# A fused attention and feed-forward kernel: two batches' state reads late, the second batch's first product kept on chip, the opening in another order

## The chip, the core and the metric

The kernel runs on one core of a Trainium2 chip. The metric is the device time of one execution in microseconds; a profiled execution also has a span, which is the time from its first to its last recorded instruction. The core has five engines, each with its own queue that runs in order: PE (matmul), DVE (VectorE), ACT (ScalarE), POOL (GpSimd) and SP, which here only issues DMA transfers.

## The reference

Both halves are in float32. For each of 8 batches and 8 heads, attention runs between 512 tokens `x` and 32 state rows, in both directions; the results, `xread` (512 rows) and `sread` (32 rows), are the input of a feed-forward layer of width 2048.

```python
scores = scale * np.matmul(x, state.transpose(0, 1, 3, 2))
scores = scores - scores.max(-1, keepdims=True)
a = np.exp(scores)
a /= a.sum(-1, keepdims=True) + 1e-09
xread = np.matmul(a, state)
scores2 = scale * np.matmul(state, x.transpose(0, 1, 3, 2))
# the same softmax over scores2 gives a2
sread = np.matmul(a2, x)
...
h = x @ w_in            # x: the (8 * 544) x 512 rows of both reads
g = h - np.tanh(h)
return g @ w_out
```

The weights arrive in float64, and the kernel takes their two 32-bit halves apart itself.

## The kernel before

**The main loop.** The rows are worked in nine chunks: chunk i below 8 is batch i's `xread`, chunk 8 is all `sread`. A chunk has 16 steps f, one for each block of 128 hidden columns: `hidden(f)` multiplies into a bank of PSUM, `finish` takes tanh on ACT and the difference on DVE and splits it into two parts `g` (the upper part by a copy on ACT, the rest by a subtraction on DVE, both in `split`, lines 90 and 91), and `output(f)` adds twelve matmuls of `g` with `wo`, the split block of `w_out` (lines 413, 414 and 415). `xread` is never formed: `m = state * w_in` is made for each batch, so that `hidden` is `a * m`.

**The products m.** For batches 0 and 1 they come from float32 matmuls with `w_in` blocks as they are converted (`m_first_two`, and letters m, k and R of the opening). The lower 64 partitions of the result are batch 0's and are copied into the SBUF tile `m_first`; the upper 64 are batch 1's and go through a tile `st` and a DMA into a DRAM tile `md`, from which `load_m` fetches them as `mr`. Batches 2 to 7 are made later, in `m_units`, and also pass through `md`.

**The weights.** Each of the 32 weight blocks (`w00d` to `w33d`, `wo0d` to `wo15d`, 512 KB each) is loaded into one of five raw tiles, converted by three DVE instructions (lines 120, 121, 124) and one on ACT (line 123), and then, for `w_out`, split (line 90 on ACT, 91 on DVE). `w_in` blocks are also written to DRAM as `wf` for later use. All loads are issued by SP, and a load waits until the conversion of an earlier block has freed its raw tile.

**The opening.** The string `SEQ` is an order written by hand. Its letters are one step each: S scores matmul, c copy of the scores to SBUF, T transpose, M maximum, B or q subtraction of the maximum (B on DVE, q on POOL), E exponential, Z, N and A normalization and transpose back, a, b, r and p the four conversion steps of a `w_in` block, m and k the product and its copy for batch 0, h and H the first hidden matmuls, X and G `finish`, D a matmul with zeros that writes nothing of use.

**State read.** `state_read(b)` computes batch b's `sread` from the copy `s` of its scores. For each half it has, on DVE, a maximum (line 306), small instructions on single columns (308, 312, 313) and four scalings (335); on ACT an exponential (310) and a copy (321); on PE four transposes (319) and its matmuls (329); on SP the load of `xn` (316).

**What sets the order elsewhere.** `SCH` is a table of step numbers st = 16 i + f: "conv", "pair" and "wo" for the weights, "a0" for batch 0's state read, "att0" and so on for the attention of later batches, "m0" and "m1" for the units of m. A planner then places instructions within an engine; `issue_after` keeps a piece from being placed ahead of another one.

Of the kernel before, what the change touches and what calls it, by code (L numbers as in the profile page):

```python
# [19 lines left out]
P = 128  # L20
# [5 lines left out]
SCALE = 1.0 / D**0.5  # L26
EPS = 1e-9
LAG = 2
LONE = 2


@with_exitstack
def attention_ffn(ctx: ExitStack, tc: tile.TileContext, xT, xn, bd, bh, sp, sm, sl, win, wout, xout, sout):
# [105 lines left out]
    WSUB = nc.gpsimd if None else None  # L139
    XSUB = nc.gpsimd if '1' else None  # L140

    def m_first_two(q, p):

        k, c = p // 2, p % 2
        if p == 0:

            m_first[q] = pool.tile([P, 2, 512], F32, tag="mr", name=f"mr0{q}", bufs=RRB)
        ps = bank(ps_a, f"mps0{q}{p}")
        nc.tensor.matmul(ps, sps[:, p], wfs[q, k][:, c], start=True, stop=True)
        nc.scalar.copy(m_first[q][64 * c : 64 * c + 64, k], ps[0:64])  # L150
        stage = pool.tile([P, 2, 512], F32, tag="stage", name=f"st0{q}{p}", bufs=SB)
        nc.scalar.copy(stage[64:128, 0], ps[64:128])
        nc.sync.dma_start(
            mdram[1][q][0][k, 2 * c : 2 * c + 2].rearrange("h n f -> (h n) f"), stage[64:128, 0]
        )

    def m_units(g):

# [33 lines left out]
                    yield  # L192

    def load_m(b, q):
        if b == 0:
            r = m_first[q]
        else:
            r = pool.tile([P, 2, 512], F32, tag="mr", name=f"mr{b}{q}", bufs=RRB)
            addends = mdram[b][q]
            nc.sync.dma_start(r, addends[0].rearrange("g h n f -> (h n) g f"))  # L200
            if len(addends) > 1:
                r2 = pool.tile([P, 2, 512], F32, tag="stage", name=f"ml{b}{q}", bufs=SB)
                nc.sync.dma_start(r2, addends[1].rearrange("g h n f -> (h n) g f"))
# [29 lines left out]
    def attention(b, aT):  # L233


        if b < LONE:
            bdr = pool.tile([P, 4, 64], F32, tag="bdr", name=f"bdr{b}", bufs=1)
        else:
            bdr = pool.tile([P, 4, NS], F32, tag="bdr", name=f"bdr{b}", bufs=1)
        with tc.issue_after(loadlog[min(len(loadlog) - 1, XH1)]):  # L240
            nc.sync.dma_start(bdr, bd[b] if b < LONE else bh[b - LONE])
        xrs, ss, es = [], [], []
        for hf in range(2):
            xr = pool.tile([P, 2, 512], F32, tag="x", name=f"xT{b}{hf}", bufs=XB)
            with tc.issue_after(loadlog[min(len(loadlog) - 1, XH1)]):
                nc.sync.dma_start(xr, xT[b, hf])
            xrs.append(xr)
        yield
        pss = {}

        def scores(hf):
            pss[hf] = bank(ps_a, f"sps{b}{hf}")
            for c in range(2):
                nc.tensor.matmul(pss[hf][64 * c : 64 * c + 64], bdr[:, 2 * hf + c], xrs[hf][:, c], start=True, stop=True)

        def all_scores():

            pss.update({hf: bank(ps_a, f"sps{b}{hf}") for hf in range(2)})
            for j in range(4):
                for hf in range(2):  # L260
                    rs = slice(64 * hf, 64 * hf + 64)
                    nc.tensor.matmul(  # L262
                        pss[hf][32 * j : 32 * j + 32], bdr[rs, j], xrs[j // 2][rs, j % 2], start=True, stop=True
                    )

        if b >= LONE:
            all_scores()
        for hf in range(2):
# [218 lines left out]
    EARLY = int('0')  # L487
# [22 lines left out]
    def step(op):  # L510
# [5 lines left out]
            for c in range(2):  # L516
                o(nc.tensor.matmul(sps_ps[j][64 * c : 64 * c + 64], bdr[:, 2 * j + c], xrs[j][:, c], start=True, stop=True))
        elif k == "c":
            ss[j] = pool.tile([P, 512], F32, tag="s", name=f"s0{j}")
            o(nc.scalar.copy(ss[j], sps_ps[j]))  # L520
        elif k == "T":
            es[j] = pool.tile([P, 512], F32, tag="e", name=f"e0{j}")
# [57 lines left out]
            chunks[0].g[j] = g  # L580
        elif k == "R":

            if j % 2 == 0:
                stages[j // 2] = pool.tile([P, 4, 256], F32, tag="stage", name=f"st00{j}", bufs=SB)
            st = stages[j // 2]
            with tc.issue_after(tanhs[RE[j]][0]):
                nc.scalar.copy(st[64:128, :, P * (j % 2) : P * (j % 2) + P], mps[j][64:128])
            if j % 2:
                for k in range(2):
                    nc.sync.dma_start(  # L590
                        mdram[1][0][0][k, :, :, P * (j - 1) : P * (j + 1)].rearrange("(c h) n f -> (h n) c f", c=2),
                        st[64:128, 2 * k : 2 * k + 2],
                    )
# [51 lines left out]
    for i in range(B + 1):  # L645
        for f in range(NFF):
# [19 lines left out]
                chunks[i + 1].hidden(nf - NFF)  # L666
            for _ in range(D0["pair"].count(st)):
                m_first_two(*next(pairs))
            with tc.issue_after(first):
                advance(a0, D0["a0"].count(st))  # L670
            for b in range(1, B):
                n = D0["att"][str(b)].count(st)
                if n:
                    if b not in atts:
                        atts[b] = new_attention(b)
                    advance(atts[b], n)
            for g in range(2):
                advance(m1[g], D0[f"m{g}"].count(st))
# [50 lines left out]
```

## Time and profile before

| what | value |
|---|---|
| device time, 3 runs | 687.70, 688.42, 689.92 us; median 688.42 |
| the profiled execution | 688.88 us, span 687.1 us, mean granted PE clock 0.988 |
| busy in the span | PE 96%, DVE 67%, ACT 55%, POOL 1% |
| DMA over the span | 99.30 MB |
| first matmul of chunk 0's output | at 32.9 us |
| last matmuls' copy out | from 683.4 us |

Matmul records overlap, so "96%" is not a rate: in the middle of the program a matmul of 512 columns starts every 0.23 us, though each record lasts 0.39. The first 140 us differ from the rest, and the views below are of that part.

### The profile page before, as it was taken

To read this page: it belongs to the slowest core of one execution; us is meant where nothing else is said; L and a number is where in the kernel's file an instruction comes from. 1 tells how busy PE (TensorE), PEld (TensorE's weight loads), DVE (VectorE), ACT (ScalarE), POOL (GpSimd) and SP (SyncE) were. 2 spreads that over 40 slices of the span, in tenths; PEclk is the share of its full clock that TensorE was granted. 3 is DMA by queue.
4 is the path that set the end of the run, shared out by engine and by line. 5 is a ranking of instruction groups with operands and counts; after the bars stand their busy time and mean duration, and the time that the engine had idled before them with its cause. 6 is when DMAs were issued, how large, how long until landed. Compare 5 with 4: busy or idle time off the path is not lost.

```text
span 687.1 us, 9286 instructions
## 1 busy us (share of the span) xinstructions
PE 660.5 (96%) x3386; PEld 521.7 (76%) x3386; DVE 458.2 (67%) x803; ACT 377.9 (55%) x663; POOL 6.6 (1%) x11
## 2 busy tenths in 40 slices
PE   4788988999999999999999999999999999999997
PEld 2446666888788887888788878887878788888896
DVE  5897999965695559556876568546853587434442
ACT  3768876766675655457656555634433354333342
POOL 2100000000000000000000000000000000000000
PEclk9899998999999999999999999999999999999999
DMA  8888972555545552345536432643241312001310
GB/s 292 252 300 257 340 275 93 183 185 144 169 122 188 150 168 97 124 126 162 175 124 203 133 106 86 220 145 127 89 157 44 124 48 95 28 14 41 131 32 31
DMA packets 46317, 99.30 MB, mean 145 GB/s; under 512 B 6208, under 2 KB 12096, under 8 KB 46272
## 3 DMA queue, kind: packets, MB, share of 16 engines
q1 hardware_dynamic: 46272, 98.72, 44.4%
q8 instruction: 26, 0.43, 0.3%
q14 instruction: 19, 0.16, 0.1%
HBM read 66.72 MB, written 31.98 MB: 144 GB/s over the span
## 4 chain that ended last, share of the span: by engine, by line
PE 85%; DMA 6%; DVE 4%; ACT 3%; issue 1%; SPq 0%; ACTq 0%; DVEq 0%
PE ops L413 17%; PE ops L414 17%; PE ops L415 17%; PE hps L376 9%; PE hps L377 9%; PE hps L375 9%; PE mps L187 2%; PE sps L262 1%; PE rps L329 1%; DMA mr<-md 1%; PE mps L186 1%; DMA w01d<-in_win 1%; DMA wf<-w 1%; PE pps L319 1%; DMA w31d<-in_win 1%; DMA wo1d<-in_wout 1%
## 5 line engine op out<-in xcount | busy, mean ns | idle before, releaser
L414 PE MATMUL ops<-wo,g 128*128 128x512 f32 x544 | 215.5, 396 | 2.1 <-DVE wo L91 2.1
L413 PE MATMUL ops<-wo,g 128*128 128x512 f32 x544 | 208.1, 397 | 3.1 <-ACT wo L90 3.1
L415 PE MATMUL ops<-wo,g 128*128 128x512 f32 x544 | 208.4, 394 | 0.0
L383 DVE TENSOR_TENSOR t<-hps,t 128x512 f32<-128x512 f32 (+1 forms) x142 | 93.3, 658 | 98.4 <-ACT t L383 97.5
L383 ACT ACTIVATE t<-hps 128x512 f32<-128x512 f32 (+1 forms) x142 | 81.1, 573 | 133.7 <-PE hps L377 131.4
L413 PEld LDWEIGHTS ops<-wo,g 128*128 128x128 f32 x544 | 102.4, 189 | 32.1 <-ACT wo L90 5.8
L90 ACT CAST g<-t 128x512 fp32r<-128x512 f32 (+1 forms) x142 | 84.6, 596 | 72.9 <-DVE t L383 56.6
L414 PEld LDWEIGHTS ops<-wo,g 128*128 128x128 f32 x544 | 103.2, 190 | 26.5 <-DVE wo L91 3.3
L91 DVE TENSOR_TENSOR g<-t,g 128x512 fp32r<-128x512 f32 (+1 forms) x142 | 93.3, 657 | 42.4 <-ACT g L90 41.1
L415 PEld LDWEIGHTS ops<-wo,g 128*128 128x128 f32 x544 | 102.8, 189 | 24.5 <-issue 2.4
L375 PE MATMUL hps<-aT,m 128*128 128x512 f32 x248 | 98.3, 397 | 0.0
L377 PE MATMUL hps<-aT,m 128*128 128x512 f32 x248 | 97.1, 393 | 0.6 <-DVE m L91 0.6
L376 PE MATMUL hps<-aT,m 128*128 128x512 f32 x248 | 97.0, 391 | 0.0
L377 PEld LDWEIGHTS hps<-aT,m 128*128 128x128 f32 x248 | 46.7, 188 | 11.0 <-DVE m L91 1.0
L91 DVE TENSOR_TENSOR wst<-w,wst 64x512 fp32r<-64x512 f32 x64 | 43.9, 686 | 16.4 <-ACT wst L90 15.0
L375 PEld LDWEIGHTS hps<-aT,m 128*128 128x128 f32 x248 | 46.6, 188 | 10.5 <-issue 0.7
L376 PEld LDWEIGHTS hps<-aT,m 128*128 128x128 f32 x248 | 46.7, 188 | 10.0 <-issue 0.5
L91 DVE TENSOR_TENSOR m<-mr,m 128x1024 fp32r<-128x1024 f32 x31 | 37.8, 1220 | 9.3 <-ACT m L90 8.6
L188 ACT COPY st<-mps 128x512 f32<-128x512 f32 x64 | 36.7, 587 | 12.3 <-PE mps L187 12.0
L90 ACT CAST wst<-w 64x512 fp32r<-64x512 f32 x64 | 39.6, 619 | 1.8 <-ACT wo13r L123 1.0
L90 ACT CAST m<-mr 128x1024 fp32r<-128x1024 f32 x31 | 32.3, 1043 | 7.3 <-DMA mr<-md 7.2
L187 PE MATMUL mps<-wst,sms 128*128 128x512 f32 x64 | 24.7, 394 | 0.0
(218 smaller groups left out, 587.6 us busy)
## 6 DMA issues: line engine op xcount, KB each, us to landing
md<-st SPq DMA_DIRECT2D x144, 128.0 KB, 2.2
mr<-md SPq DMA_DIRECT2D x28, 512.0 KB, 4.0
xT<-in_xT SPq DMA_DIRECT2D x16, 512.0 KB, 4.6
xn<-in_xn SPq DMA_DIRECT2D x16, 512.0 KB, 4.2
w<-wf SPq DMA_DIRECT2D x16, 512.0 KB, 4.6
out_x<-ob SPq DMA_DIRECT2D x32, 256.0 KB, 2.1
wn<-wf SPq DMA_DIRECT2D x8, 512.0 KB, 3.8
ml<-md SPq DMA_DIRECT2D x8, 512.0 KB, 3.6
```

The costliest lines, as they stand in the source:

```text
L90: nc.scalar.copy(hi, src)
L91: return (sub or nc.vector).tensor_sub(lo, src, hi)
L186: nc.tensor.matmul(ps, s[:, 1, h], t[:, e], start=True, stop=False)
L187: nc.tensor.matmul(ps, s[:, 0, h], t[:, e], start=(g == 1), stop=True)
L188: nc.scalar.copy(stage[:, e], ps)
L375: nc.tensor.matmul(ps, mhi[k][:, cols], ahi[:, k], start=(k == 0), stop=False)
L376: nc.tensor.matmul(ps, mhi[k][:, cols], alo[:, k], start=False, stop=False)
L377: nc.tensor.matmul(ps, mlo[k][:, cols], ahi[:, k], start=False, stop=(k == nk - 1))
L383: tanhs.append((nc.scalar.activation(t, ps, AF.Tanh).ins, nc.vector.tensor_sub(t, ps, t).ins))
L413: nc.tensor.matmul(o, g[:, 0, tok], wo[:, f, 0], start=(f == 0), stop=False)
L414: nc.tensor.matmul(o, g[:, 0, tok], wo[:, f, 1], start=False, stop=False)
L415: return nc.tensor.matmul(o, g[:, 1, tok], wo[:, f, 0], start=False, stop=(f == NFF - 1)).ins
```

## The change

1. **Late state reads.** Attention of batches 0 and 1 (`EARLY_S`) keeps its scores in tiles of their own, and `state_read` for them runs at steps 58 to 64 ("a0") and 74 to 80 ("r1"), in chunks 3 to 5, where it was in chunk 0 before.
2. **Second batch on chip.** The upper 64 partitions of the first products are copied into an SBUF tile `m_second`, and `load_m` uses it; `st`, the DMA to `md` and back are gone for batch 1. For q = 0 and 1 this tile takes the place of a "stage" tile, and "m0" starts at step 16, not 11.
3. **POOL's part.** Both subtractions of the maximum in the opening (q becomes B) and both differences of batch 0's split `aT` run on DVE.
4. **Order.** `w00d` is loaded ahead of `bd` and `x`, `SEQ` is new (one D fewer), only batch 0 uses the wide form of the scores (`LONE` is 1), and up to step 47 attention and units of m are placed after the tanh and difference of that step (`GATED`).

The state read has the same arithmetic as before, in its narrow form (w = 1) for all batches.

```diff
-LONE = 2
+GATED = 48
+EARLY_S = 2
+LONE = 1
...
+    def second(q):
+        if q < 2:
+            return pool.tile([P, 2, 512], F32, tag="stage", name=f"mr1{q}", bufs=SB)
+        return pool.tile([P, 2, 512], F32, tag=f"mr1{q}", name=f"mr1{q}", bufs=1)
...
             m_first[q] = pool.tile([P, 2, 512], F32, tag="mr", name=f"mr0{q}", bufs=RRB)
+            m_second[q] = second(q)
         ps = bank(ps_a, f"mps0{q}{p}")
         nc.tensor.matmul(ps, sps[:, p], wfs[q, k][:, c], start=True, stop=True)
         nc.scalar.copy(m_first[q][64 * c : 64 * c + 64, k], ps[0:64])
-        stage = pool.tile([P, 2, 512], F32, tag="stage", name=f"st0{q}{p}", bufs=SB)
-        nc.scalar.copy(stage[64:128, 0], ps[64:128])
-        nc.sync.dma_start(
-            mdram[1][q][0][k, 2 * c : 2 * c + 2].rearrange("h n f -> (h n) f"), stage[64:128, 0]
-        )
+        nc.scalar.copy(m_second[q][64 * c : 64 * c + 64, k], ps[64:128])
...
-        if b == 0:
-            r = m_first[q]
+        if b < 2:
+            r = (m_first, m_second)[b][q]
...
-            s = pool.tile([P, 512], F32, tag="s", name=f"s{b}{hf}")
+            s = pool.tile([P, 512], F32, tag=f"s{b}{hf}" if b < EARLY_S else "s", name=f"s{b}{hf}", bufs=1 if b < EARLY_S else 2)
...
-        yield from state_read(b, ss)
+        if b >= EARLY_S:
+            yield from state_read(b, ss)
+        else:
+            late[b] = ss
...
+    def split_first():
+        for hf in range(2):
+            split(aTs[0][:, 0, hf], aTs[0][:, 1, hf], ats[hf])
...
-        if b == 0:
-            for hf in range(2):
-                split(aTs[0][:, 0, hf], aTs[0][:, 1, hf], ats[hf], nc.gpsimd if P0[4] else None)
...
-            w = 2 if b < LONE else 1
+            w = 1
...
-    load(EARLY)
+    load(1)
     nc.sync.dma_start(bdr, bd[0])
     for hf in range(2):
         nc.sync.dma_start(xrs[hf], xT[0, hf])
     nc.sync.dma_start(sps, sp)
-    load(5 - EARLY)
+    load(4)
...
-    SEQ = 'S0 c0 T0 S1 D D M0 c1 q0 a0 r1 T1 D D r0 a1 E0 M1 b0 q1 E1 p0 D Z0 b1 D N0 Z1 p1 A0 N1 m0 k0 D m1 a2 k1 A1 r2 a3 h0 H0 h1 H1 b3 b2 p2 X0 G0 X1 m2 r3 D p3 m3 k2 D G1 k3'
+    SEQ = 'a0 r0 b0 p0 S0 c0 T0 S1 D D M0 c1 B0 T1 E0 D D M1 B1 a1 r1 E1 b1 m0 k0 p1 Z0 N0 D A0 m1 k1 Z1 N1 D A1 a2 r2 h0 H0 h1 H1 b2 X0 p2 G0 X1 m2 a3 r3 b3 p3 D m3 k2 D G1 k3'
...
-"a0": [0, 0, 1, 13]
+"a0": [58, 60, 62, 64]
...
-"m0": [11, 11, 15, 15, 20, 21, 21, 22, 22, 23, 25, 27, 29, 33, 35, 36]
+"m0": [16, 17, 18, 19, 20, 21, 21, 22, 22, 23, 25, 27, 29, 33, 35, 36]
...
+"r1": [74, 76, 78, 80]
...
-            with tc.issue_after(first):
+            with ExitStack() as gates:
+                if st < GATED:
+                    for x in tanhs[st]:
+                        gates.enter_context(tc.issue_after(x))
                 advance(a0, D0["a0"].count(st))
-            for b in range(1, B):
...
+                advance(late1, D0["r1"].count(st))
+                for b in range(1, B):
```

The table's entries are shown without the rest of their line, and the loop's new indentation is left out. Where the rows below name lines, the change's line numbers are 4 to 17 higher.

DVE's queue from its first instruction, before (`e` are the scores being turned into weights, `w` a weight block in conversion, `m` the maximum):

```order
L523 STREAM_TRANSPOSE e_152<-s_150 128x512
L526 TENSOR_REDUCE m_159<-e_152 128x16
L120 TENSOR_SCALAR w_164<-w00d 128x512
L523 STREAM_TRANSPOSE e_169<-s_161 128x512
L120 TENSOR_SCALAR w_164<-w01d 128x512
L526 TENSOR_REDUCE m_176<-e_169 128x16
L121 SCALAR_TENSOR_TENSOR w_164<-w00d,w_164 128x512
L124 ISA w_164<-w_164,w00r 128x1024
```

and with the change:

```order
L124 TENSOR_SCALAR w_139<-w00d 128x512
L125 SCALAR_TENSOR_TENSOR w_139<-w00d,w_139 128x512
L128 ISA w_139<-w_139,w00r 128x1024
L539 STREAM_TRANSPOSE e_153<-s_151 128x512
L542 TENSOR_REDUCE m_160<-e_153 128x16
L544 TENSOR_TENSOR e_153<-e_153,m_160 128x512
L539 STREAM_TRANSPOSE e_165<-s_162 128x512
L542 TENSOR_REDUCE m_170<-e_165 128x16
L544 TENSOR_TENSOR e_165<-e_165,m_170 128x512
```

The whole conversion of `w00d` now stands ahead of the first transpose of scores, and the two subtractions (L544) are new in this queue.

DVE's queue a little later, from the first difference of chunk 0's `g` to the subtraction that completes `wo`'s block 0, before:

```order
L576 TENSOR_TENSOR g_0_242<-t_0_239,g_0_242 128x512
L569 TENSOR_TENSOR t_1_245<-hps_1_230,t_1_245 128x512
L306 TENSOR_REDUCE m_358<-s_150 128x1
L306 TENSOR_REDUCE m_438<-s_161 128x1
L124 ISA w_217<-w_217,w03r 128x1024
L120 TENSOR_SCALAR w_292<-w10d 128x512
L124 ISA wor_282<-wor_282,wo0r 128x1024
L308 TENSOR_SCALAR nm_360<-m_358 128x1
L576 TENSOR_TENSOR g_1_267<-t_1_245,g_1_267 128x512
L308 TENSOR_SCALAR nm_440<-m_438 128x1
L121 SCALAR_TENSOR_TENSOR w_292<-w10d,w_292 128x512
L120 TENSOR_SCALAR wor_329<-wo1d 128x512
```

and with the change:

```order
L592 TENSOR_TENSOR g_0_230<-t_0_223,g_0_230 128x512
L125 SCALAR_TENSOR_TENSOR wor_276<-wo0d,wor_276 128x512
L125 SCALAR_TENSOR_TENSOR w_286<-w11d,w_286 128x512
L585 TENSOR_TENSOR t_1_233<-hps_1_219,t_1_233 128x512
L124 TENSOR_SCALAR w_212<-w03d 128x512
L128 ISA wor_276<-wor_276,wo0r 128x1024
L125 SCALAR_TENSOR_TENSOR w_212<-w03d,w_212 128x512
L128 ISA w_212<-w_212,w03r 128x1024
L124 TENSOR_SCALAR w_286<-w10d 128x512
L592 TENSOR_TENSOR g_1_258<-t_1_233,g_1_258 128x512
L95 TENSOR_TENSOR wo<-wor_276,wo 128x512
```

The maxima of the state read (L306, L308) are gone from here, and `wo0` is completed before the next block's conversion starts. Counted from the start to the subtraction that completes `wo15`, DVE's queue had 226 instructions and has 198.

PE's queue between the second and third group of `wo` matmuls, before (`pps` and `rps` are the state read's, `mps` the products m):

```order
L415 MATMUL ops_3_392<-wo,g_1_267 128x512
L319 MATMUL pps_369<-ident,s_150 128x128 x4
L329 MATMUL rps_376<-xn_367,p2t_374 64x128 x8
L149 MATMUL mps_432<-w_321,sps 128x512
L413 MATMUL ops_0_389<-wo,g_2_345 128x512
```

and with the change:

```order
L432 MATMUL ops_3_346<-wo,g_1_258 128x512
L161 MATMUL mps_386<-w_312,sps 128x512
L161 MATMUL mps_497<-w_402,sps 128x512
L392 MATMUL hps_4_431<-aT_116,m_428 128x512
```

The state read's transposes and matmuls stand here no longer; they follow in chunks 3 to 5.

More of the change, by code (lines that the diff above doesn't have):

```diff
@@ L72, in attention_ffn @@
         [[dram.tile([2, 4, NS, 512], F32, name=f"md{b}{q}{i}") for i in range(1 if b < 6 else 2)] for q in range(NQ)]
+        if b >= 2
+        else None
         for b in range(B)
@@ L140, in attention_ffn @@
     XSUB = nc.gpsimd if '1' else None
+    m_second = {}
+    def second(q):
+        if q < 2:
+            return pool.tile([P, 2, 512], F32, tag="stage", name=f"mr1{q}", bufs=SB)
+        return pool.tile([P, 2, 512], F32, tag=f"mr1{q}", name=f"mr1{q}", bufs=1)
     def m_first_two(q, p):
@@ L295, in attention, with late_read @@
             yield split(aT[:, 0, hf], aT[:, 1, hf], at)
-        yield from state_read(b, ss)
+        if b >= EARLY_S:
+            yield from state_read(b, ss)
+        else:
+            late[b] = ss
+    late = {}
+    def late_read(b):
+        yield from state_read(b, late[b])
+    def split_first():
+        for hf in range(2):
+            split(aTs[0][:, 0, hf], aTs[0][:, 1, hf], ats[hf])
     def state_read(b, ss):
-        if b == 0:
-            for hf in range(2):
-                split(aTs[0][:, 0, hf], aTs[0][:, 1, hf], ats[hf], nc.gpsimd if P0[4] else None)
         for hf in range(2):
@@ L486, in attention_ffn @@
     xrs = [pool.tile([P, 2, 512], F32, tag="x", name=f"xT0{hf}", bufs=XB) for hf in range(2)]
-    EARLY = int('0')
-    load(EARLY)
+    load(1)
     nc.sync.dma_start(bdr, bd[0])
@@ L498, in attention_ffn @@
     m_first[0] = pool.tile([P, 2, 512], F32, tag="mr", name="mr00", bufs=RRB)
-    wb, stages, mps, sps_ps, hps, ss = {}, {}, {}, {}, {}, {}
+    wb, mps, sps_ps, hps, ss = {}, {}, {}, {}, {}
     es, ms, zs = {}, {}, {}
@@ L518, in step @@
         elif k == "c":
-            ss[j] = pool.tile([P, 512], F32, tag="s", name=f"s0{j}")
+            ss[j] = pool.tile([P, 512], F32, tag=f"s0{j}", name=f"s0{j}", bufs=1)
             o(nc.scalar.copy(ss[j], sps_ps[j]))
@@ L581, in step @@
         elif k == "R":
-            if j % 2 == 0:
-                stages[j // 2] = pool.tile([P, 4, 256], F32, tag="stage", name=f"st00{j}", bufs=SB)
-            st = stages[j // 2]
+            if j == 0:
+                m_second[0] = second(0)
             with tc.issue_after(tanhs[RE[j]][0]):
[L587 to L593, printed above, removed]
+                for c in range(2):
+                    nc.scalar.copy(m_second[0][64 * c : 64 * c + 64, :, j * P : j * P + P], mps[j][64:128, c::2])
     MP = [{"a": ps_a, "o": ps_o}[x] for x in 'oaoa']
     RE = json.loads('[1, 0, 0, 1]')
-    SEQ = 'S0 c0 T0 S1 D D M0 c1 q0 a0 r1 T1 D D r0 a1 E0 M1 b0 q1 E1 p0 D Z0 b1 D N0 Z1 p1 A0 N1 m0 k0 D m1 a2 k1 A1 r2 a3 h0 H0 h1 H1 b3 b2 p2 X0 G0 X1 m2 r3 D p3 m3 k2 D G1 k3'
+    SEQ = 'a0 r0 b0 p0 S0 c0 T0 S1 D D M0 c1 B0 T1 E0 D D M1 B1 a1 r1 E1 b1 m0 k0 p1 Z0 N0 D A0 m1 k1 Z1 N1 D A1 a2 r2 h0 H0 h1 H1 b2 X0 p2 G0 X1 m2 a3 r3 b3 p3 D m3 k2 D G1 k3'
     for op in SEQ.split():
@@ L605, in attention_ffn @@
     a0 = state_read(0, ss)
+    split_first()
+    late1 = late_read(1)
     with tc.issue_after(afters[FILL[0]]):
@@ L617, in attention_ffn @@
     atts = {}
-    SCH = dict(json.loads('{"conv": [0, 1, 2, 2, 3, 3, 4, 4, 6, 7], "pair": [0, 1, 3, 3, 3, 3, 4, 5, 6, 7], "a0": [0, 0, 1, 13], "att0": [3, 5, 7, 7, 7, 8, 9, 11, 13], "att1": [6, 7, 8, 8, 11, 11, 11, 11, 13], "att2": [5, 9, 9, 13, 13, 13, 13, 13, 13], "m0": [11, 11, 15, 15, 20, 21, 21, 22, 22, 23, 25, 27, 29, 33, 35, 36], "m1": [40, 46, 52, 53, 53, 54, 55, 57, 62, 62, 62, 65, 73, 77, 79, 84], "wo": [0, 1, 2, 3, 4, 5, 6, 7, 8, 8, 9, 9, 10, 10, 12]}'))
+    SCH = dict(json.loads('{"conv": [0, 1, 2, 2, 3, 3, 4, 4, 6, 7], "pair": [0, 1, 3, 3, 3, 3, 4, 5, 6, 7], "a0": [58, 60, 62, 64], "att0": [3, 5, 7, 7, 7, 8, 9, 11, 13], "att1": [6, 7, 8, 8, 11, 11, 11, 11, 13], "att2": [5, 9, 9, 13, 13, 13, 13, 13, 13], "m0": [16, 17, 18, 19, 20, 21, 21, 22, 22, 23, 25, 27, 29, 33, 35, 36], "m1": [40, 46, 52, 53, 53, 54, 55, 57, 62, 62, 62, 65, 73, 77, 79, 84], "wo": [0, 1, 2, 3, 4, 5, 6, 7, 8, 8, 9, 9, 10, 10, 12], "r1": [74, 76, 78, 80]}'))
     D0 = dict(
@@ L668, in attention_ffn @@
                 m_first_two(*next(pairs))
-            with tc.issue_after(first):
+            with ExitStack() as gates:
+                if st < GATED:
+                    for x in tanhs[st]:
+                        gates.enter_context(tc.issue_after(x))
                 advance(a0, D0["a0"].count(st))
-            for b in range(1, B):
[L672 to L678, printed above, removed]
+                advance(late1, D0["r1"].count(st))
+                for b in range(1, B):
+                    n = D0["att"][str(b)].count(st)
+                    if n:
+                        if b not in atts:
+                            atts[b] = new_attention(b)
+                        advance(atts[b], n)
+                for g in range(2):
+                    advance(m1[g], D0[f"m{g}"].count(st))
             chunks[i].output(f)
@@ L713 @@
     win, wout = (c(w).view(np.int64) if w.dtype == np.float64 else w for w in (moe_w_in, moe_w_out))
-    nc = bacc.Bacc("TRN2", target_bir_lowering=False, num_devices=1)
+    nc = bacc.Bacc("TRN2", target_bir_lowering=False, num_devices=1, dynamic_dma_scratch_size=1024)
     arrays = {"in_xT": xT, "in_xn": xn, "in_bd": bd, "in_bh": bh, "in_sp": sp, "in_sm": sm, "in_sl": sl, "in_win": win, "in_wout": wout}
```

## Prediction

> **What bounds the kernel now.** I read the page's slices first, then the engines' busy time by stretch, then the waits of PE and DVE in the first 140 us, and last the chain of waits around 138 us.
>
> ```profile
> PE   4788988999999999999999999999999999999997
> DVE  5897999965695559556876568546853587434442
> PEclk9899998999999999999999999999999999999999
> ```
>
> Each digit is 17 us. From the eighth slice on PE is full, and DVE is near full only in the first eight. So the program has two parts: an opening in which something else sets the pace, and some 550 us in which PE does. What the change can win lies in the opening; afterwards it can only move PE work about. Cut at useful places, DVE's queue looks like this (stretch, length, DVE busy and instructions, granted PE clock, DMA share and GB/s; the last row adds up all engines to 138.3 us):
>
> ```profile
> 0.00:7.78 7.78, 0.00 (x0) 1.00 0.71 233
> 7.78:34.60 26.82, 23.87 (x44) 0.87 0.89 284
> 34.60:76.60 42.00, 36.66 (x71) 0.96 0.89 299
> ...
> sum 138.30, PE 115.38 PEld 78.24 DVE 120.66 ACT 95.11 POOL 6.60; mean PE 28.84 PEld 19.56 DVE 30.16 ACT 23.78 POOL 1.65
> ```
>
> Up to 138.3 us DVE is busy for 120.7 and idle for 17.6: 7.8 before its first instruction, 3.0 up to 34.6, 5.3 up to 76.6, then 1.6. That point is the end of the subtraction that completes the last weight block, `wo15`; PE starts the matmuls of that step just before it and from there has its weights ready:
>
> ```profile
> 137.51 0.68 DVE L91 TENSOR_TENSOR wo<-wor,wo 128x512 fp32r<-128x512 f32 x1
> 137.48 0.91 PE ops L413 x4
> PE ops L413 <- ACT wo L90: 3.1, 3, 1.7
> 138.30:660.00 521.70, 521.70 (x2769) 1.00 0.39 123
> ```
>
> PE's waits for `wo` are in the opening, and the last row shows no idle time from 138.3 to 660. ACT has 95 us of work up to there and DVE 121, so DVE sets the pace: **the end moves with the time at which DVE gets through this queue, plus whatever PE work is moved behind that point.** DVE's idle times are for the most part these:
>
> ```profile
> DVE e L523 <- ACT s L520: 7.8, 1, 7.8
> DVE wor L120 <- DMA wo1d<-in_wout: 2.2, 1, 2.2
> DVE wor L120 <- DMA wo4d<-in_wout: 1.1, 1, 1.1
> DVE w L120 <- DMA w31d<-in_win: 1.1, 1, 1.1
> DVE w L120 <- PE mps L149: 1.0, 1, 1.0
> DVE wor L120 <- DMA wo5d<-in_wout: 0.6, 1, 0.6
> ```
>
> **The change part by part.** First, DVE's work up to `wo15`. The state reads of two batches leave it:
>
> ```profile
> 27.28 1.27 DVE L306 TENSOR_REDUCE m<-s 128x1 f32<-128x512 f32 x2
> 133.19 1.15 DVE L335 TENSOR_SCALAR sr<-rps,ri 32x64 f32<-32x64 f32 x4
> 109.12 0.68 DVE L121 SCALAR_TENSOR_TENSOR wor<-wo11d,wor 128x512 uint32<-128x512 uint32 x1
> 107.65 0.16 DVE L313 RECIPROCAL ri<-ri 128x1 f32<-128x1 f32 x1
> 37.05 0.69 DVE L383 TENSOR_TENSOR t<-hps,t 128x512 f32<-128x512 f32 x1
> ```
>
> Four maxima are two pairs of 1.27 us, 2.5; sixteen scalings are four groups of 1.15, 4.6; twelve instructions on single columns at up to 0.16, which overlap their neighbours, about 0.8: 7.9 in all, and I take 7.6 since the groups overlap the next instruction too. Four subtractions come over from POOL. DVE's own differences of two 128x512 tiles take 0.69, so these add 2.7. The other moves of the new order (one `g`, one `m` more ahead of the point, two `wst` fewer) add about 0.5. Net **-4.4**. In chunks 3 to 5, to which the reads go, DVE is at 4 to 8 tenths and has room for 7.6 us.
>
> Second, POOL and DVE slow each other. Of DVE's conversions those that overlap a POOL instruction are long:
>
> ```profile
> 11.68 1.42 POOL L528 TENSOR_TENSOR e<-e,m 128x512 f32<-128x512 f32 x1 [1.20 <-DVE m L526]
> 12.34 1.31 DVE L124 CUSTOM_DVE_ANT_0 w<-w,w00r 128x1024 uint16<-128x1024 uint16 x1
> 23.00 0.69 DVE L124 CUSTOM_DVE_ANT_0 w<-w,w02r 128x1024 uint16<-128x1024 uint16 x1
> 19.59 0.87 DVE L120 TENSOR_SCALAR w<-w03d 128x512 uint32<-128x512 uint32 x1
> 18.63 0.42 DVE L120 TENSOR_SCALAR w<-w02d 128x512 uint32<-128x512 uint32 x1
> 21.11 1.75 DVE L121 SCALAR_TENSOR_TENSOR w<-w02d,w 128x512 uint32<-128x512 uint32 x1
> ```
>
> 1.31 against 0.69, 0.87 against 0.42 and 1.75 against 0.68: 0.6 + 0.5 + 1.1 = 2.2. POOL has none of this work any more: **-2.2**. Bounds: 0, if these were long for another reason, and 2.2.
>
> Third, the head. One weight block ahead of `x` delays it by what the queue takes for a block:
>
> ```profile
> 2.60 0.49 SPq L109 DMA_DIRECT2D w00d<-in_win  x1
> 3.13 0.60 SPq L109 DMA_DIRECT2D w01d<-in_win  x1
> w00d<-in_win SPq DMA_DIRECT2D x1, 512.0 KB, 6.5
> w01d<-in_win SPq DMA_DIRECT2D x1, 512.0 KB, 7.4
> DMA to landing us min/median/max: 3.8/4.5/5.2
> ```
>
> `w00d` landed at 2.60 + 6.5 = 9.1 and `w01d` at 3.13 + 7.4 = 10.5, so a block costs 1.4 us, and the first transpose of scores moves from 7.8 to 9.2. In return `w00d`, now issued first, lands at about 0.7 + 3.8 = 4.5 (an estimate from the faster of the two `xT` loads, the last row), and its three conversions, 0.42 + 0.68 + 0.69 less their overlap, 1.6 in all, are done before the scores come. Later and earlier cancel: -0.2, with a wait of 0.3 for `w01d` that goes as well, **-0.4**. If `w00d` took its old 6.5, it would land at 7.2 and the conversions would still end at 8.8, before 9.2.
>
> Fourth, DVE's waits for transfers and others, 2.2 for `wo1d` and 5.3 between 34.6 and 76.6. The change takes 16 `md` writes (128 KB), 3 `mr` reads and 4 `xn` loads (512 KB each) out of the first 112 us, some 6 MB of 30.6, and the DMA share there is 0.89, so transfers land sooner. But DVE comes sooner too, and the raw tiles are freed only by DVE and ACT; a load still takes about 5 us from issue to landing:
>
> ```profile
> DMA packets 13369, 30.57 MB, mean 273 GB/s; under 512 B 1200, under 2 KB 6192, under 8 KB 13362
> md<-st SPq DMA_DIRECT2D x16, 128.0 KB, 4.7
> ```
>
> In front of `wo1d` stood two `md` issues; without them, and with 0.26 MB (0.9 us at 284 GB/s) less in the queue, half the wait should go: -1.1. Between 34.6 and 76.6 ten `md` writes, 1.3 MB, are 4.4 us of the queue at 299 GB/s; I take back a quarter of the waits, **-1.3**, since the faster DVE eats the rest. Bounds for the two together: from 0 wait left, -7.5, to all that DVE saves given back, +6.6.
>
> DVE is through at 138.3 - 4.4 - 2.2 - 0.4 - 1.1 - 1.3 = **128.9, that is 9.4 earlier.**
>
> Fifth, PE's work behind that point. Half a batch's state read is, in the part where PE is full:
>
> ```profile
> 348.27 0.44 PE pps L319 x4
> 354.88 0.58 PE rps L329 x32
> ```
>
> 1.02 us. All four halves were ahead of `wo15`'s matmuls and are now behind: +4.1. The new order has 8 other matmuls (6 `hps`, 2 `mps`) ahead of the point that were behind it, at 0.91 / 4 = 0.23 (the row of four `ops` above): -1.8. Net **+2.3**. The narrow scores of batch 1 and the missing zero matmul lie in the opening, under DVE, and count nothing there; without that cover they would be worth under 1 us.
>
> The reads' ACT work (four exponentials, four copies) and `xn` loads go where DMA's share is 0.39 on average and ACT, busy for 55% of the span, has room; batches 2 to 7 have the same reads there and PE has no idle time. The copies into `m_second` are as many as those into `st`.
>
> Sum: -9.4 + 2.3 = -7.1. The profiled execution took 688.88 (span 687.1, and 1.8 around it), 0.46 above the median of the runs shown. Predicted: 688.88 - 7.1 = **681.8 us**.
>
> [...] PE's clock falls to half around the end of the opening:
>
> ```profile
> 112.00:118.00 6.00, 5.81 (x14) 0.50 0.26 87
> ```
>
> For 6 us PE is busy at half the clock, which loses 3.0. Here it is covered, since DVE comes to `wo15` only 20 us later. If the change's DVE is faster but PE has its gaps at the same places, such a stretch may fall where PE sets the end: +3.0. [...]
>
> **The rivals.** (a) *The waits vanish.* With 6 MB less, loads could be ahead of DVE throughout: the 1.1 and 4.0 us that I left also go, 681.8 - 5.1 = 676.7. For it: the DMA share of 0.89. Against it: the raw tiles, and waits for PE and ACT among them.
>
> (b) *The ring of raw tiles sets the pace.* Five tiles of 5 us latency feed DVE; what DVE saves (4.4 + 2.2) it waits for blocks instead, and the two gains on waits fail. Then only 0.4 is left against PE's +2.3, and some of this is covered: 689 to 690.8, about the same as before. For it: 2.8 us of the middle waits (`wo4d`, `w31d`, `wo5d`) are for blocks. Against: most of DVE's queue, 36.7 of 42.0, was busy.
>
> (c) *Half clock where PE is bound*: 681.8 + 3.0 = 684.8, as above.
>
> (d) *Slower: late reads stop PE.* `xn` and `xT` share two tiles, and at steps 58 to 80 eight half reads (batches 0 and 1 beside 4 and 5) pass through them, with SP's queue in order: an `xn` that waits for its tile holds the loads of `mr` behind it, and PE waits in order. A load takes 4.2:
>
> ```profile
> xn<-in_xn SPq DMA_DIRECT2D x16, 512.0 KB, 4.2
> ```
>
> At 1.5 us exposed for each of the eight reads this is 12 us: 693.8. It decides against the change from 0.9 us a read. Against it: a step lasts over 4 us (128 steps in the 546 us from 137.5 to the last copy out), the reads are two steps apart, and the same reads of batches 2 to 7 cost no PE idle time.
>
> That the change does not do what it says I rule out: the queues shown have the reads moved and no `md` of batch 1.
>
> **How the numbers follow.** Chances: forecast 0.56, (a) 0.12, (b) 0.12, (c) 0.10, (d) 0.10. The forecast's own range is 679 to 685: its waits 3 us either way. The range for 8 in 10 leaves out (d) and half of (a) and goes up into (b): 677.5 to 689. A change of under 0.3%, 2.1 us, cannot be told from none. Faster: forecast, (a), (c), less their edges, 0.77; same: (b), 0.13; slower: (d), 0.10.
>
> **What would show it.** In the changed profile: DVE's first instruction at 4 to 5 us and its first transpose at about 9; no POOL work after the first 2 us; no conversion of over 0.7; `wo15` completed at 127 to 131; waits of DVE after its start of 5 to 7 us; no PE idle time from there to 660, the rows of chunks 3 to 5 included. It is wrong if DVE's waits grow to over 12 (b), or if PE waits for `xn`, `p2t` or `mr` behind 240 us (d).

## The result, and the profile after

The changed kernel takes **681.95 us** (median of 4 runs, 680.73 to 683.06), the kernel before in the same session 689.17 (687.7 to 691.78). The ratio is 0.9896, with a 95% interval from 0.9867 to 0.9924: 7.2 us faster, where the executions of the kernel before lie within 4.1 us. 681.8 was forecast. The profiled execution took 682.26 us with a span of 680.4.

The slices of the page, as before 17 us each:

```profile
PE   5779999999999999999999999999999999999997
DVE  5889999965966459756966488547854687444442
PEclk9889989999999999999999999999999999999999
```

In both kernels DVE falls to 6 tenths in the ninth slice; PE is at 9 tenths or more from the fourth slice up to the last, where it was from the eighth. DVE's queue cut at the same kind of places (start and end, length, each engine's busy time with its instructions, granted clock, DMA share, GB/s):

```profile
0.00:9.20 9.20, 2.63 (x8) 0.70 (x8) 1.82 (x4) 2.54 (x3) 1.17 (x7) 1.00 0.75 264
9.20:34.75 25.55, 18.95 (x75) 11.41 (x72) 22.69 (x41) 16.12 (x34) 0.00 (x0) 0.93 0.69 214
34.75:76.60 41.85, 37.95 (x141) 24.05 (x140) 38.80 (x69) 34.61 (x60) 0.00 (x0) 0.96 0.84 296
76.60:127.48 50.88, 46.77 (x192) 36.34 (x191) 50.50 (x87) 37.46 (x63) 0.00 (x0) 0.97 0.45 149
sum 127.48, PE 106.31 PEld 72.50 DVE 113.81 ACT 90.73 POOL 1.17; mean PE 26.58 PEld 18.12 DVE 28.45 ACT 22.68 POOL 0.29
```

DVE is the third of the five. It was busy for 113.8 us up to the completion of `wo15`, and idle for 7.4 + 2.9 + 3.0 + 0.4 = 13.7. The same cut of the kernel before is one row:

```profile
0.00:138.19 138.19, 120.55 (x227) 0.94 0.74 248
```

So that point came 10.7 earlier (138.2 to 127.5): 6.7 are less work, 4.0 less waiting. On DVE and PE the point itself and its neighbour look like this in the changed kernel:

```profile
126.79 0.69 DVE L95 TENSOR_TENSOR wo<-wor,wo 128x512 fp32r<-128x512 f32 x1
126.95 1.07 PE L430 MATMUL ops<-wo,g 128*128 128x512 f32 x4
```

Some of what DVE (first three rows, up to 127.5) and PE (behind 138) still wait for:

```profile
DVE e L539 <- ACT s L536: 2.4, 1, 2.4
DVE wor L124 <- DMA wo1d<-in_wout: 1.3, 1, 1.3
DVE wor L124 <- DMA wo2d<-in_wout: 1.3, 1, 1.3
PE hps L392 <- DVE t L400: 0.3, 1, 0.3
```

PE has 0.3 us of idle time in more than 540 us: nothing of the late reads stops it.

### The profile page after: what moved, and what is told of

It is laid out like the page before. It is cut to its first block, busy times and chain, and to the rows that moved or that the text cites. A ratio compares the mean times of both kernels' runs of the same rounds, so it can differ in the third digit from the quotient of the medians.

```text
span 680.4 us, 9375 instructions
## 1 busy us (share of the span) xinstructions
PE 655.5 (96%) x3456; PEld 518.1 (76%) x3456; DVE 459.1 (67%) x807; ACT 378.2 (56%) x667; POOL 1.2 (0%) x7
## 4 chain that ended last, share of the span: by engine, by line
PE 83%; DVE 8%; DMA 5%; ACT 2%; issue 1%; SPq 0%; ACTq 0%; DVEq 0%
PE ops L430 17%; PE ops L431 16%; PE ops L432 16%; PE hps L392 9%; PE hps L393 9%; PE hps L394 9%; PE mps L195 2%; DMA wf<-w 1%; PE rps L346 1%; PE sps L270 1%; DMA wo6d<-in_wout 1%; PE pps L336 1%; PE mps L194 1%; DMA wo2d<-in_wout 1%; DVE wor L125 1%
```

## The experiments

All twelve do the whole of the kernel's work. Eight change one thing in the source, after which the planner places the instructions anew, so that the order on every engine differs from the changed kernel's. The last four have an order written down and enforced (the changed kernel's, in pin_other that of p_act), so that an edit is measured without this. "wo15" is the time of that completion in the profile; busy and idle are DVE's up to there. A profile is one execution and can lie 1 to 2 us from the median (p_dma's took 687.94, ring6's 685.76, u_pool's 682.98), so these three columns can be off by as much.

| run | edit to the changed kernel | us | ratio to before, 95% | wo15 | busy | idle |
|---|---|---|---|---|---|---|
| the changed kernel | | 681.95 | 0.9896 [0.9867, 0.9924] | 127.5 | 113.8 | 13.7 |
| u_reads | state reads back in chunk 0 | 686.73 | 0.9967 [0.9951, 0.9984] | 138.5 | 124.1 | 14.5 |
| u_dram | batch 1 through DRAM | 685.31 | 0.9944 [0.9927, 0.9962] | 131.6 | 116.0 | 15.6 |
| u_pool | four subtractions on POOL | 681.73 | 0.9887 [0.9862, 0.9913] | 128.4 | 113.1 | 15.3 |
| u_first | w00d behind x | 686.24 | 0.9952 [0.9933, 0.9972] | 133.3 | 115.5 | 17.8 |
| p_dve | six more subtractions, DVE | 685.94 | 0.9934 [0.9910, 0.9958] | 131.6 | 117.2 | 14.4 |
| p_act | six more copies, ACT | 680.78 | 0.9866 [0.9847, 0.9885] | 125.8 | 113.5 | 12.3 |
| p_dma | twelve more writes | 686.13 | 0.9948 [0.9931, 0.9965] | 132.1 | 113.8 | 18.3 |
| ring6 | a sixth raw tile | 684.60 | 0.9921 [0.9890, 0.9952] | 130.2 | 113.5 | 16.7 |
| pin_dma | p_dma, order held | 686.04 | 0.9962 [0.9945, 0.9979] | 131.7 | 113.9 | 17.8 |
| pin_first | u_first, order held | 684.07 | 0.9929 [0.9905, 0.9954] | 129.8 | 113.7 | 16.1 |
| pin_pool | u_pool, order held | 681.99 | 0.9903 [0.9883, 0.9923] | 127.5 | 113.1 | 14.4 |
| pin_other | order of p_act, no copies | 682.29 | 0.9909 [0.9888, 0.9929] | 128.3 | 114.1 | 14.2 |

Differences below are between medians. The kernel before had medians from 688.55 to 689.72 in the different sessions; by the ratios, which allow for that, the differences come out within 1 us of these, except for p_dve (2.6 us for 4.0). Only u_reads, u_dram, u_first, p_dma and pin_dma have an interval that does not overlap the changed kernel's.

**Does DVE set the pace, and ACT not?** Six subtractions (p_dve) or copies (p_act) of a tile that nothing else uses, one in each of steps 1 to 6:

```diff
+            if 1 <= st <= 6:
+                with tc.issue_after(tanhs[st][1]):
+                    nc.vector.tensor_sub(dum2, dum, dum)
...
+                with tc.issue_after(tanhs[st][0]):
+                    nc.scalar.copy(dum2, dum)
```

> The changed kernel with six needless DVE subtractions of 128x512 tiles in steps 1 to 6 of chunk 0 (their result is not used). Theory: DVE sets the opening, so all six lie on the path: wo15 4.1 us later, at 131.5, and the time 4 us more, 686. Rival (transfers): the added work fills DVE's waits for blocks, 3 us of them, and costs 1 us or less. Rival (PE): no change.

> The changed kernel with six needless ACT copies of 128x512 tiles in steps 1 to 6 of chunk 0. Theory: ACT was idle for 36 of the first 127 us, so 3.6 us more cost little: wo15 0 to 1 us later, time 682 to 683. Rival (ACT's copies are on the path to each step's g and wo, as PE's waits for wo's upper half name ACT): 3.6 us more, 685.6.

Six operations of 0.68 us on DVE moved wo15 by 4.1 and the median by 4.0 (the profiles' spans, 680.4 and 684.5, differ by 4.1 too); the same number on ACT cost nothing. So DVE is on the path, in the profiles at a slope of one, and ACT is not. The runs with late reads say the same: from `wo15` to the end of the span are 552.9 us in the changed kernel and 551.8 to 554.1 in the other eleven profiles with late reads, while `wo15` goes from 125.8 to 133.3.

**The late reads.** u_reads puts both batches' reads back to where batch 0's were:

```diff
-EARLY_S = 2
+EARLY_S = 0
...
-"a0": [58, 60, 62, 64]
+"a0": [0, 0, 1, 13]
```

(the entry "r1" is empty, and batch 1's read follows its attention).

> The changed kernel with both state reads back in chunk 0, all else as changed. Theory (DVE's queue up to wo15 sets the opening, PE the rest): DVE has 7.6 us more ahead of wo15, which moves from 127.5 to about 135, and PE has some 4 us less behind it: 682.0 + 7.6 - 4.1 = 685.5. Rival (transfers set the opening): only the four xn loads, 2 MB, come back, wo15 moves by 0 to 2 us, and with 4 us less PE work behind it the kernel is faster, 678 to 680.

4.8 us are lost, two thirds of the whole gain, with wo15 at 138.5 where the theory had 135. DVE's busy time to wo15 grows by 10.3, of which the reads are these rows of the kernel before (grouped by line, up to 138.2; count, busy and mean ns), and some 0.8 of small instructions:

```profile
L335 DVE TENSOR_SCALAR sr<-rps,ri 32x64 f32<-32x64 f32 x16 | 4.5, 278 | 0.2
L306 DVE TENSOR_REDUCE m<-s 128x1 f32<-128x512 f32 x4 | 2.6, 660 | 0.0
```

Less what overlaps their neighbours, these are 7.4. Two subtractions for `wst` that the planner now placed ahead of the point are 1.4 more; the last 1.5 is for the most part less overlap between other instructions. In u_reads PE's matmuls of step 15 start here:

```profile
137.00 0.84 PE L430 MATMUL ops<-wo,g 128*128 128x512 f32 x3
```

From there to the end of the span are 684.6 - 137.0 = 547.6 us; in the changed kernel 680.4 - 126.95 = 553.5. So a step 15 that starts 10.0 us earlier was bought with 5.9 us more behind it, and the difference, 4.2 in these two profiles, is the gain.

**The second batch on chip.** u_dram restores `st`, the writes to `md` and the reads as `mr` for batch 1. p_dma keeps the product on chip and only adds twelve writes of it that nobody reads:

```diff
         nc.scalar.copy(m_second[q][64 * c : 64 * c + 64, k], ps[64:128])
+        nc.sync.dma_start(dram.tile([64, 512], F32, name=f"xd{q}{p}"), m_second[q][64 * c : 64 * c + 64, k])
```

> The changed kernel with batch 1's product through st, a DMA to md and back as before, all else as changed. Theory: DVE's work is the same; 16 more writes and 4 more reads lengthen some of its waits; wo15 at 127.5 to 129.5, time 682 to 684. Rival (transfers set the opening): 4 of the 6 MB taken off come back and with them most of the gain: wo15 at 132 or later, time 686 to 688.

> The changed kernel with twelve needless 128 KB writes of batch 1's product to DRAM, in the places where they stood before; nothing reads them. Theory: 1.6 MB more in the queue lengthen DVE's waits a little: wo15 0 to 1.5 us later, time 682 to 683.5. Rival (transfers set the opening): 1.6 MB at 296 GB/s are 5.3 us, time 687.

u_dram lost 3.4 us, with wo15 at 131.6: neither the theory's 682 to 684 nor the rival's 686 to 688, but nearer to the rival. p_dma, with DVE's work unchanged, lost as much as 4.2, which the theory had not expected of 1.6 MB in a queue that moves about 300 GB/s (296 in the changed kernel from 34.75 to 76.60 us). Since the order had changed too, the same writes were tried in the changed kernel's own order; only SP's queue then has twelve rows more:

```diff
+    for name, places in order.items():   # the changed kernel's order on PE, DVE, ACT and SP
...
+        row = [mine[k] for k in places]
+        for x, y in zip(row, row[1:]):
+            tc.add_manual_dep(y, x.name, ...)
```

> The changed kernel's order of instructions on PE, DVE and ACT, instruction for instruction, and on SP twelve needless writes of 128 KB of the second batch's product to DRAM beside it (results unused). Theory now (the 4.2 us of the earlier run with these writes came for the most part from the different order that came with them): wo15 completed within 1.5 us of 127.5, 682 to 683.5 us. Rival (the transfers themselves delay the loads, 12 x 0.44 us of the DMA queues): wo15 at 131 to 132 and 686 us.

The rival was right: 686.04 us, wo15 at 131.7. The writes do it, but not by their bytes alone. DVE's waits up to there, grouped, in pin_dma:

```profile
DVE w L124 <- issue: 2.5, 1, 2.5
DVE wor L124 <- DMA wo2d<-in_wout: 2.1, 1, 2.1
DVE w L124 <- DMA w31d<-in_win: 0.6, 1, 0.6
```

The 2.5 are new, and the profile names no releaser for them. `w22d` is converted into one of two tiles, and the tile's last use is the write of the converted `w12d` and `w13d` to DRAM (`wf<-w`). The rows of DVE, ACT and SP around it in pin_dma, and what its DMA issues took to land (its lines are up to 2 higher):

```profile
43.12 0.68 DVE L128 CUSTOM_DVE_ANT_0 w<-w,w13r 128x1024 uint16<-128x1024 uint16 x1
...
47.26 0.58 ACT L164 COPY mr<-mps 64x512 f32<-64x512 f32 x1
...
47.87 0.45 SPq L165 DMA_DIRECT2D xd<-mr  x1
48.41 0.54 SPq L482 DMA_DIRECT2D wf<-w  x1
...
wf<-w SPq DMA_DIRECT2D x1, 512.0 KB, 3.7
...
52.18 0.43 DVE L124 TENSOR_SCALAR w<-w22d 128x512 uint32<-128x512 uint32 x1 [2.46 <-issue]
```

and in the changed kernel:

```profile
43.85 0.33 SPq L480 DMA_DIRECT2D wf<-w  x1
...
48.80 0.42 DVE L124 TENSOR_SCALAR w<-w22d 128x512 uint32<-128x512 uint32 x1
```

The block was ready at 43.8 in both. In the changed kernel its write is issued at once. With the extra writes, one of them stands ahead of it in SP's queue and waits for a copy that ACT ends at 47.8; the `wf` write is issued 4.6 us late, lands at 48.4 + 3.7 = 52.1, and DVE starts at 52.2. That is 2.5 of the 4.1. Of the rest, 0.9 is the wait for `wo2d` (2.1 against 1.3), which lands 7.5 us after its issue where it took 6.7, with two of the writes issued just behind it; 0.6 is a new wait for `w31d`. A small write whose source comes late is thus paid for by what stands behind it in the queue. u_dram has the same pattern (a write of `st` issued at 45.0, `wf` at 45.5), but its time is mixed: idle time +1.9, work ahead of the point +2.2, and PE's work behind it about 1 less.

**The raw tiles.** ring6 gives the weight blocks a sixth tile (`PB` 4 for 3), without which rival (b) cannot be judged.

> The changed kernel with six raw tiles for weight blocks in place of five. Theory: DVE's waits for blocks after its start (wo1d 1.3, wo2d 1.3, wo6d 0.5) go, as loads are issued earlier: wo15 about 3 us earlier, time 679 to 680. Rival (the queue of transfers is full, so an earlier issue only waits longer): no change.

Neither came: its median is 2.6 us higher, though the intervals overlap. Its waits of DVE for blocks behind the start are

```profile
DVE wor L124 <- DMA wo1d<-in_wout: 0.8, 1, 0.8
DVE wor L124 <- DMA wo3d<-in_wout: 0.3, 1, 0.3
```

1.1 behind the head, where the changed kernel has 3.1 (1.3, 1.3 and 0.5 for `wo6d`): the tile did what it could. But in the order planned for it waits for ACT and a wait without a named releaser, as in pin_dma, came up instead, and DVE's idle time rose by 3.0. The clock differs as well: in this profile it is at half from 16.2 to 26.5 us, in the changed kernel's from 21.1 to 24.5. Held to the changed kernel's order it was not tried. What a sixth tile is worth by itself stays open.

**`w00d` first.** u_first loads it behind `x`; pin_first does so in the order of the changed kernel:

```diff
-    load(1)
...
-    load(4)
+    load(5)
```

> The changed kernel with w00d loaded behind x, as before; the steps' order is the new one, so DVE waits for w00d ahead of the scores. Theory: x comes 1.4 us earlier, but the first block's 1.6 us of conversion now stand behind its later landing (9 us), ahead of the scores: the first transpose at 10.5 to 11 where it was 9.2, wo15 1 to 2 us later, 683 to 684. Rival (only the scores' way counts at the head): x earlier, 680.6.

> The changed kernel's order on PE, DVE and ACT, with w00d loaded behind bd, x and sps. The first three conversions on DVE then wait for w00d, and the transpose of the scores stands behind them. Theory: first transpose at 11.4 where it was 9.2, of these 2.2 us about 1.5 to 2.2 reach wo15: 683.5 to 684.5 us. Rival 1 (the earlier run of this edit, 686.2, was all the load's place): 686. Rival 2 (the waits further back take it up): 682.

In a fixed order the load's place is worth 2.1 us (684.07; the interval overlaps the changed kernel's, but the profile agrees); u_first lost 4.3, more than its theory had, and the other 2.2 came with its new order. In pin_first DVE's first rows are

```profile
9.36 0.43 DVE L124 TENSOR_SCALAR w<-w00d 128x512 uint32<-128x512 uint32 x1 [9.36 <-DMA w00d<-in_win]
...
11.27 0.70 DVE L539 STREAM_TRANSPOSE e<-s 128x512 f32<-128x512 f32 x1
```

so the first transpose is 2.1 later than in the changed kernel (9.2), and wo15 2.3.

**POOL.** u_pool and pin_pool move the four subtractions back (B to q for the maximum, and the differences of `aT`):

```diff
-            split(aTs[0][:, 0, hf], aTs[0][:, 1, hf], ats[hf])
+            split(aTs[0][:, 0, hf], aTs[0][:, 1, hf], ats[hf], nc.gpsimd)
```

> The changed kernel with the two subtractions of the maximum and the two differences of aT on POOL again. Theory: DVE has four instructions less, -2.7, and loses 2.2 to POOL's overlap: wo15 within 1 us of 127.5, time within 1 us of 682.0. Rival (the long conversions had another reason): nothing is lost to overlap, wo15 at 124.8, time 679.3. Second rival (POOL's 1.2 to 1.5 us for each on the way to the first hidden matmul): the first output matmul starts 1 us or more later than 30.9 and the time is 683 or more.

> The changed kernel's order on PE and ACT, DVE's without its four subtractions, which run on POOL. Theory: DVE saves 2.7 us of work and loses about 2.2 to conversions that run beside POOL; within 1 us of 682. Rival 1 (no such contention): wo15 at 124.8 and 679.3. Rival 2 (POOL's 1.4 us against DVE's 0.7 lies in the chain from scores to weights): 683 to 685.

No difference in either (681.73, 681.99). In pin_pool DVE's work falls by 0.7 only, not by the 2.7 of the four subtractions, because what runs beside POOL is longer:

```profile
12.13 1.16 POOL L545 TENSOR_TENSOR e<-e,m 128x512 f32<-128x512 f32 x1 [0.31 <-DVE m L543]
12.42 1.42 DVE L125 SCALAR_TENSOR_TENSOR w<-w01d,w 128x512 uint32<-128x512 uint32 x1
...
17.96 1.26 POOL L95 TENSOR_TENSOR aT<-at,aT 128x512 fp32r<-128x512 f32 x1 [4.67 <-ACT aT L94]
18.32 1.44 DVE L554 TENSOR_TENSOR e<-e,z 128x512 f32<-128x512 f32 x1
```

1.42 and 1.44 where these take 0.69, which is 1.5 of the missing 2.0; the last 0.5 is spread over small differences. POOL's subtraction beside the 1.42 took 1.16, the one ahead of it, beside DVE rows of 0.69 and 0.71, 1.05. The 0.7 went into waits (14.4 for 13.7). Giving DVE this work cost nothing and won nothing.

**What the parts do not add up to.** Taken back one at a time, the reads are worth 4.8, the second batch on chip 3.4, POOL's part nothing and the load of `w00d` 2.1: 10.3 for a change that gained 7.2. So the parts cannot be added. No run takes back the new `SEQ`, `GATED`, `LONE` or the value of `dynamic_dma_scratch_size`, which the change also sets, so what these are worth is not shown.

**Order or chance?** p_act was 1.2 us faster than the changed kernel, though it does more. pin_other takes its order and leaves the six copies out.

> The changed kernel's work, nothing added or left out, in the order that was planned for the kernel with six needless copies on ACT (without those copies). Theory (placing the same work otherwise is worth 1 us and more): 679.5 to 681, wo15 at 125.5 to 126.5. Rival (the 1.2 us of that kernel were chance): 682, wo15 at 127.5.

682.29, as the rival had it (wo15 at 128.3, not 127.5): by itself the order is worth nothing that can be told from none. In these two profiles, p_act's and the slowest of pin_other's four executions, the kernels part in the first matmuls of chunk 0, ahead of the first of the six copies (27.9). PE from 15 to 27 us in p_act (start, length, line, matmuls, and the wait ahead), with the granted clock from 20 to 25 us (last number but two in the last row):

```profile
15.37 1.16 PE L573 MATMUL mps<-w,sps 128*128 128x128 f32 x8 [1.79 <-DVE w L128]
...
18.02 1.10 PE L581 MATMUL hps<-at,mr 128*128 128x512 f32 x2 [1.06 <-ACT w02r L127]
20.94 4.35 PE L581 MATMUL hps<-at,mr 128*128 128x512 f32 x6 [1.82 <-DVE at L556]
...
20.00:25.00 5.00, 4.06 (x6) 0.66 0.32 97
```

and in pin_other from 12 us, with the clock from 14 to 17, 17 to 20 and 20 to 25:

```profile
12.79 0.60 PE L530 MATMUL warm<-blank 128*128 128x256 f32 x2
15.40 1.16 PE L574 MATMUL mps<-w,sps 128*128 128x128 f32 x8 [2.02 <-DVE w L128]
...
18.06 2.04 PE L582 MATMUL hps<-at,mr 128*128 128x512 f32 x2 [0.89 <-ACT w02r L127]
20.98 5.49 PE L582 MATMUL hps<-at,mr 128*128 128x512 f32 x6 [0.88 <-DVE at L557]
...
14.00:17.00 3.00, 1.59 (x10) 0.95 1.02 291
17.00:20.00 3.00, 2.11 (x3) 0.50 0.55 178
20.00:25.00 5.00, 4.12 (x6) 0.50 0.31 88
```

The clock fell to half in both: in p_act from 20.6 for 3.4 us, in pin_other from 16.7 for 10.2 and once more from 30.3 for 3.4. Eight matmuls took 7.5 us instead of 5.5, chunk 0's first output matmul came at 34.6 instead of 32.2, and wo15 2.5 later. That p_act's lead is chance is not shown by this: its four executions (680.1 to 681.62) all lie below pin_other's four (681.76 to 683.02), and the two intervals do not overlap. It goes with the clock, and why the clock was kinder to p_act stays open. p_act is not kept as a better version: its interval overlaps the changed kernel's.

## Why the prediction was right

**The frame held.** "The end moves with the time at which DVE gets through this queue, plus whatever PE work is moved behind that point": from `wo15`'s completion -10.7 and +4.0 (548.9 to 552.9 us from there to the end of the span), against -9.4 and +2.3. Both terms were too small by 1.3 to 1.7, and the errors cancel in the sum (-6.7 in the profiles, -7.1 forecast). So the 681.8 is better than its terms, and that it hit to 0.2 us is luck. One profile stands for each kernel here, while executions of one kernel differ by 2 to 4 us.

**DVE's work**, -6.6 forecast, -6.7 measured. Reads -7.4 for -7.6; four subtractions +2.7 for +2.7; conversions that no longer run beside POOL -2.0 for -2.2; the other moves -0.1 for +0.5. These were counts times durations from rows, and all but the small last one came out. On ACT, "as many as those into `st`" is four copies short: for q = 0 eight copies of 0.37 us stand where four of 0.58 did.

**The waits**, -2.8 forecast (head -0.4, `wo1d` -1.1, the middle -1.3), -4.0 measured. The head gave -0.4: 7.4 idle for 7.8. From there to 34.7 the waits fell by 0.1 only (3.0 to 2.9): `wo1d` went from 2.2 to 1.3 and the 0.3 for `w01d` went, but a wait of 1.0 for chunk 0's first tanh is new, and the forecast has no such term. That tanh comes behind matmuls at half clock. In the changed kernel (first row) these six start at 20.95 and take 4.54 us; in u_dram's profile (second row), where the clock stayed full there, they start at 20.97, take 2.84, and the wait is 0.8 shorter:

```profile
23.58 0.69 DVE L585 TENSOR_TENSOR t<-hps,t 128x512 f32<-128x512 f32 x1 [1.05 <-ACT t L584]
22.77 0.69 DVE L586 TENSOR_TENSOR t<-hps,t 128x512 f32<-128x512 f32 x1 [0.21 <-ACT t L585]
```

The stretch from 34.6 to 76.6 gave -2.3 (5.3 to 3.0), and behind it, where nothing was forecast, 1.2 (1.6 to 0.4). The step that was mis-sized is "I take back a quarter of the waits": it counted the `md` writes as bytes in the transfer queue. pin_dma shows that in the changed kernel such writes can cost more by their place in SP's queue, 2.5 of 4.1 us in one wait. That this is what the change took away is not shown: in the kernel before the `wf` write was issued at 43.0, and no wait for it followed in DVE's queue.

**PE's work behind the point**, +2.3 forecast, +3.7 measured: from the start of step 15's matmuls to the end of the span 687.1 - 137.31 = 549.8 us before and 553.5 now. (From `wo15`'s completion it is +4.0, as PE started that step 0.9 us ahead of it and now starts 0.5 ahead.) In the kernel before they start here, in the same view as the row at 126.95 above (the prediction's 137.48 is from another view, in which the changed kernel has 127.11):

```profile
137.31 1.07 PE L413 MATMUL ops<-wo,g 128*128 128x512 f32 x4
```

The counts came out: behind that start are 16 transposes and 128 matmuls of the reads more, and 6 `hps` and 2 `mps` fewer. "1.02 us" for half a read was the length of the reads' own matmuls. The rows of a late read in the changed kernel show that their neighbours pay too:

```profile
182.84 0.39 PE L432 MATMUL ops<-wo,g 128*128 128x512 f32 x1
183.07 0.60 PE L336 MATMUL pps<-ident,s 128*128 128x128 f32 x4
183.42 0.48 PE L392 MATMUL hps<-aT,m 128*128 128x512 f32 x1
183.74 0.40 PE L393 MATMUL hps<-aT,m 128*128 128x512 f32 x1
...
199.72 0.39 PE L432 MATMUL ops<-wo,g 128*128 128x512 f32 x1
200.04 0.65 PE L346 MATMUL rps<-xn,p2t 128*32 128x64 f32 x32
200.62 0.50 PE L194 MATMUL mps<-wst,sms 128*128 128x512 f32 x1
200.96 0.40 PE L195 MATMUL mps<-wst,sms 128*128 128x512 f32 x1
```

From 182.84 to 183.74 are 0.90 us, less two ordinary matmuls at 0.23 leaves 0.44; from 199.72 to 200.96 are 1.24, less two leaves 0.78. That makes 1.22 a half and 0.8 more for four. The wait of 0.3 for `t` is new as well. That leaves 0.3 of the 1.4 unexplained.

**The rivals.** (a), no waits left, is out: 6.3 us of waits remain behind the first transpose's start. (b) is out too, in the size that it had: the waits fell. (c), half clock where PE is bound, did not happen behind `wo15`; the stretch at 112 to 118 went, and another came at 86 to 90 us, where it is as well covered (DVE reaches `wo15` 37 us later):

```profile
86.00:90.00 4.00, 3.73 (x10) 0.58 0.76 258
```

In the first 35 us it is not covered: there DVE's queue itself waits for PE, as the 1.0 above shows.

(d) is out by PE's 0.3 us of idle time.

**What would show it**: the first DVE instruction at 4.8 and the first transpose at 9.2 (4 to 5 and 9), no POOL work after 2 us, conversions of at most 0.71, `wo15` at 127.5 (127 to 131), waits of 6.3 us after the first transpose's start (5 to 7), and 0.3 us of PE idle time in place of none. Two things that are not on the list mattered in the experiments: the order in SP's queue and the clock in the first 35 us.

## What to carry to other kernels

Find the instruction after which the full engine never waits again (here `wo15`: PE has 0.3 us of idle time behind it). Work on the engine that leads to it then moved that point in full (six subtractions of 0.68 us, 4.1), work that was pushed behind it was paid on the other side (3.7), and the difference was the gain. Price a moved piece by start-to-start times that include its neighbours (here 1.22 for half a read), not by its own records (1.02). Price a small transfer first by what stands behind it in the issuing queue, should its source be late (in pin_dma a `wf` write issued 4.6 us late and a wait of 2.5), and only then by its bytes.

## What was not expected of the hardware

**Half clock although PE works for part of the time.** In pin_other PE ran dry at 12.79 + 0.60 = 13.4, waited 2.02 us, and was at half clock from about 16.7 (0.95 on average over 14 to 17 leaves 0.3 us at 0.50). In p_act a wait of 1.79 at the same place left the clock alone, but the waits of 1.06 and 1.82 behind it did not: half clock from 20.6. In u_dram's profile the same three places have waits of 1.06, 1.06 and 1.82, and the clock stayed full up to 39 us; in the changed kernel one of 2.15, ahead of 28.96, left it alone. So the length of one wait does not decide. In the traces of the kernel before and of the changed kernel, from 8 to 130 us, six stretches of half clock last 3.41 us and one lasts 6.83, and those of one trace begin on marks that are multiples of 3.41 us apart and lie elsewhere in the other: at 19.0, 29.3, 53.2 and 111.2 us before, at 21.1, 41.6 and 86.0 with the change. Between two marks at full clock PE's records covered 1.44 us or less six times, and half clock followed each time; it also followed once on 1.93, did not follow on 1.59 (once in each trace), and never followed on 2.07 or more. In pin_other they covered 1.39 of the 3.41 up to 16.7; in p_act, with its marks 0.5 us further on, 1.59 up to 17.2 and 1.10 up to 20.6. What sets the marks is not shown.

**A lower clock goes with a longer time.** The four executions of the changed kernel took 680.73 us at a mean granted clock of 0.995, 681.64 and 682.26 at 0.992, and 683.06 at 0.985; those of p_act 680.1 to 681.62 at 0.995 to 0.997, of pin_other 681.76 at 0.992 and 682.26 to 683.02 at 0.987. So a lower clock goes with most of the 2.3 us by which the executions of the changed kernel differ. That it is the cause was not tested by an experiment of its own.
